# Channel mixing's moving operands placed at multiples of 64 bytes, weights left 32 bytes off, and GpSimd's first loads one head pair later

## The chip, the cores and the metric

The kernel runs on one core of a Trainium2 chip. The metric is the device time of one execution in microseconds (us). TensorE (PE in the profile) multiplies: a weight load (LDWEIGHTS, PEld in the profile) brings the stationary operand into the array, and a matmul streams the moving operand past it, one column after the other. VectorE (DVE), ScalarE (ACT) and GpSimd (POOL) do elementwise work; SyncE (SP) issues DMA transfers, and so do GpSimd and ScalarE. Tiles lie in SBUF, where each of the 128 partitions has its own bytes; an address here means the byte offset within a partition. Matmul results go to PSUM.

## The reference

All inputs and the output are float64 or float32 arrays that the kernel reads as 32-bit words; shapes are batch 4, 12 heads of 64, sequence 448, width 768.

```python
scores = q @ k^T / 8 - log(448)                  # sigmoid attention, per head
x  = sigmoid(scores) @ v                         # heads side by side: 4 x 448 x 768
u  = x + (x^T @ U @ V)^T                         # token mixing of rank 32
u  = u + relu(u @ w_ch1) @ w_ch2                 # channel mixing, 768 -> 3072 -> 768
th = u @ w_theta
u2 = u + w_tok_r @ (u * cos(th)) + w_tok_i @ (u * sin(th))
out = u2 + relu(u2 @ w_ch)
```

## The kernel before, in words

**Arithmetic.** Most products use float32r operands split into a high and a low part, and each product is three matmuls: high by high, high by low, low by high.

**Attention (lines 592 to 647).** The loop over `p` handles 24 pairs of heads. `load_qk(p)` fetches a pair's q and k in four quarters each, `TK(p)` and `TQ(p)` transpose them on DVE into `kT_t[p]` and `qT_t[p]`, `K_hi`, `K_lo` and the function that `TQ` returns split them. `QK(p, c)` makes three chunks of scores (9 matmuls for each of two heads, side by side in the array), ACT takes the sigmoid, `AV` multiplies by v (in plain float32), `QK_rest` and `AV_rest` do the 64 keys left over, once per two pairs. `load_qk(p + 4)` at the end of a turn keeps q and k four pairs ahead. All these q and k transfers but the first pair's are issued by SP.

**Early conversion.** Meanwhile ten float64 matrices of the later stages are loaded on GpSimd's queue and converted to float32 in small steps: `esteps` lists all steps of all jobs in order, 48 in all, and `early_step()` does the next one. The order of the jobs is that of the `queue(...)` calls (lines 495 to 504): U0, V0, one block of w_ch1, U1, V1, one of w_ch2, and four more weight blocks. Before a job's first step (`size`, line 139) the load of the job two places further on is issued. The first two loads are issued in the loop at `p == 0`, behind a small copy on GpSimd that reads `kT_t[1]` and so holds GpSimd until that transpose is done (line 606). Calls of `early_step` begin at `p == 1`: two in each turn, and one more in turns 4 and 6.

**Channel mixing (from line 652).** It goes over 12 blocks `i` of the hidden width and 4 batches `b`. `ch1(i, b)` (lines 664 to 666) has the weights `w1` stationary and `uh`, `ul` (the split u) moving, 448 columns; `ch2(i, b)` (lines 686 to 688) has `w2` stationary and `gh`, `gl` (the split hidden layer) moving, 448 columns. Each has 36 matmuls, and each matmul has a weight load of its own. The matmuls of one `ch2` run behind the `ch1` of the next batch, so that ACT and DVE have time to make `gh` and `gl`.

**Where the tiles lie.** Pools are stacks: left pools grow upward from low addresses, right ones downward from the top. The allocator gives each tile a multiple of 32 bytes. Every large tile here has a size that is a multiple of 256 bytes, so a pool's start fixes the place of all its tiles relative to lines of 64 bytes. `X` begins at 17088, a multiple of 64. The small tile `warm` behind it takes 32 bytes, so that the weight rings of `wpool` begin at 60128, which is 32 past a multiple of 64, and so does every tile of the left pools above it: `cv` (conversion), `gpool` (`gh`, `gl` from 121568), the attention pools `ap`, `ap1`, `ap2`, then `u23` (`uh`, `ul` of batches 2 and 3 from 135904) and `sp`. The right stack ends at 229344, also 32 past a multiple, and `u01` (`uh`, `ul` of batches 0 and 1, from 186336) lies there. So in the kernel before each moving operand and each stationary one of attention, channel mixing and the stages behind it starts 32 bytes past a multiple of 64; matmul operands at multiples of 64 are those of the transposes alone (`X`, `ident`).

Of the kernel before, what the change touches and what calls it, by code (L numbers as in the profile page):

```python
# [11 lines left out]
F32 = mybir.dt.float32  # L12
# [12 lines left out]
def tile_kernel(  # L25
# [15 lines left out]
    nc = tc.nc  # L41
# [4 lines left out]
    P = 128  # L46
# [23 lines left out]
    def runs(b, n0, n1):  # L70

        if b % 2 == 0:
            return [(n0, n0, n1 - n0)]
        got = []
        if n0 < REM:
            e = min(n1, REM)
            got.append((n0, n0 + S - REM, e - n0))
            n0 = e
        if n0 < n1:
            got.append((n0, n0 - REM, n1 - n0))  # L80
        return got
# [19 lines left out]
    def pool(name, side="left", space=None):  # L101
        st = ExitStack()
        kw = dict(name=name, bufs=1, side=side, reuse_waits="tile")
        if space is not None:
            kw["space"] = space
        return st.enter_context(tc.tile_pool(**kw)), st


    def hi_act(o, i):
        nc.scalar.activation(o, i, AF.Copy)  # L110
# [7 lines left out]
    def lo_dve(o, i, h):  # L118
        nc.vector.tensor_sub(o, i, f(h))
# [63 lines left out]
    def fin_split(dest, key, name, tag):  # L183
        def fin(a, t):
            dest[key] = ring(tag, name)
            split(dest[key], a, lo_pool if "sp" in late else lo_dve)
        return fin

    def loader():
        return nc.sync if "sp" in late else nc.gpsimd  # L190

    def load_row(src, r0):
        def dma(s):
            loader().dma_start(out=s.rearrange("p n t -> p (n t)"), in_=src[r0:r0 + P, :])
        return dma

    def conv_w1(i, j):
        c0 = (i * FB + j) * P

        def dma(s):  # L200
            loader().dma_start(
                out=s.rearrange("p (k f) t -> p k (f t)", k=NK),
                in_=w1_w[:, 2 * c0:2 * (c0 + P)].rearrange("(k p) f -> p k f", p=P),
            )
        return Conv(f"w1_{i}_{j}", P, DM, dma, fin_split(w1_t, (i, j), f"w1_{i}_{j}", "w1"))

    def conv_w2(i, j):
        name = f"w2_{i}_{j}"
        return Conv(name, P, DM, load_row(w2_w, (i * FB + j) * P), fin_split(w2_t, (i, j), name, "w2"))
# [56 lines left out]
    def conv_U(par):  # L266
        def dma(s):
            sv = s.rearrange("p (k r) t -> p k (r t)", k=NS)
            for g in range(P // R):
                for n, t, m in runs(par, 0, S):  # L270
                    nc.gpsimd.dma_start(
                        out=sv[g * R:(g + 1) * R, n // R:(n + m) // R],
                        in_=U_w[t:t + m, :].rearrange("(k j) w -> j k w", j=R),
                    )

        def dest():
            return u_in[:, par].rearrange("p k r -> p (k r)").bitcast(U32)
        return Conv(f"U{par}", P, NS * R, dma, None, dest=dest)

    def conv_V(par):  # L280
        def dma(s):
            sv = s.rearrange("p n t -> p (n t)")
            for g in range(P // R):
                for n, t, m in runs(par, 0, S):
                    nc.gpsimd.dma_start(
                        out=sv[g * R:(g + 1) * R, 2 * n:2 * (n + m)], in_=V_w[:, 2 * t:2 * (t + m)]
                    )

        def fin(a, t):
            hi_act(vh[:, par], a)  # L290
            lo_dve(vl[:, par], a[:2 * R], vh[:2 * R, par])
        return Conv(f"V{par}", P, S, dma, fin)

    cv, cv_st = pool("cv")
    gpool, gpool_st = pool("gpool")
    late = {}

# [64 lines left out]
    kT_t, qT_t = {}, {}  # L362

    def TK(p):
        x = ap2.tile([P, S], F32, tag="kT", name=f"kT_{p}", bufs=2)
        nc.vector.transpose(out=x, in_=k_t.pop(p).rearrange("p k j -> p (k j)"))
        kT_t[p] = x
# [4 lines left out]
    def K_hi(p):  # L372
        h_ = ap2.tile([P, NFULL, P], F32R, tag="kh", name=f"kh_{p}", bufs=2)
        l_ = ap2.tile([P, NFULL, P], F32R, tag="kl", name=f"kl_{p}", bufs=2)
        kk_t[p] = (h_, l_)
        hi_act(h_, by_chunks(p))
# [10 lines left out]
    def QK(p, c):  # L387
        ps = ps_b.tile([P, 2, 512], F32, tag="sc", name=f"sc_{p}_{c}", bufs=2)[:, :, :S]
        (kh, kl), (qh, ql) = kk_t[p], qq_t[p]
        for n, (a, b) in enumerate(((kh, qh), (kh, ql), (kl, qh))):  # L390
            for h in range(2):
                sl = slice(h * D, (h + 1) * D)
                nc.tensor.matmul(ps[:, h], a[sl, c], b[sl], start=n == 0, stop=n == 2)  # L393
        A_t[p, c] = weigh(ps, "A", f"A_{p}_{c}", 4)
# [94 lines left out]
    def queue(name, job):  # L489
        if seq:  # L490
            seq[-1].next = job
        seq.append(job)
        plan[name] = job

    queue("U0", conv_U(0))
    queue("V0", conv_V(0))
    queue(("w1", 0, 0), conv_w1(0, 0))
    queue("U1", conv_U(1))
    queue("V1", conv_V(1))
    queue(("w2", 0, 0), conv_w2(0, 0))  # L500
    queue(("w1", 0, 1), conv_w1(0, 1))
    queue(("w2", 0, 1), conv_w2(0, 1))
# [56 lines left out]
    warm = cpool.tile([P, 1], F32, name="warm")  # L559
# [22 lines left out]
    def split_u(b, p, d0, d1, *los):  # L582
        if d0 == 0:
            uh_t[b] = p.tile([P, NK, S], F32R, name=f"uh{b}")
            ul_t[b] = p.tile([P, NK, S], F32R, name=f"ul{b}")
        for d in range(d0, d1):
            x = X[:, d, b * S:(b + 1) * S]
            hi_act(uh_t[b][:, d], x)
            los[d % len(los)](ul_t[b][:, d], x, uh_t[b][:, d])
# [8 lines left out]
    for p in range(NP):  # L598
        nx = p + 1 < NP
        QK(p, 0)  # L600
        QK(p, 1)
        if nx:
            TK(p + 1)
            TQ(p + 1)()
        if p == 0:
            nc.gpsimd.tensor_copy(warm, kT_t[1][:, :1])
            seq[0].load()
            seq[1].load()
        if p:
            AV(p - 1, 0)  # L610
            AV(p - 1, 1)
        if nx:
            K_hi(p + 1)
        if p:
            early_step()
        if nx:
            K_lo(p + 1)
        b, r = divmod(p - 2 - NH, NH)
        if b >= 0 and r == 0:
            U1(b, ap)  # L620
            u1_lo()
        b, r = divmod(p - 3 - NH, NH)
        if b >= 0 and r < NK // 2:
            ps = ps_a.tile([P, 2, 512], F32, tag="ux", name=f"h_{b}_{r}")
            U2(b, 2 * r, ps, (vh[:, b % 2], vl[:, b % 2]))
        QK(p, 2)
        if not nx:
            ap2_st.close()
            u01, u01_st = pool("u01", "right")
            split_u(0, u01, 0, 3, lo_dve)  # L630
        if p % 2 == 0:
            QK_rest(p // 2)
        if p:
            AV(p - 1, 2)
        if p % 2:
            AV_rest(p // 2)
        if p > 1:
            XT(p - 2)
        if p in (4, 6):
            early_step()  # L640
        if p % 2 == 0 and p + 2 < NP:
            load_v(p // 2 + 1)
        if p + 4 < NP:
            load_qk(p + 4)
        if p:
            early_step()
    split_u(0, u01, 3, NK, lo_dve)
    while esteps:
# [6 lines left out]
    def ch1(i, b, js=range(FB)):  # L655
        if js[0] == 0:
            g_t[i, b] = ps_g.tile([P, FB, 512], F32, tag="g", name=f"g_{i}_{b}", bufs=2)
        ps = g_t[i, b]
        for j in js:
            wh, wl = w1_t[i, j][:, 0], w1_t[i, j][:, 1]  # L660
            for kk in range(NK):
                o = ps[:, j, :S]
                sl = slice(kk * P, (kk + 1) * P)
                nc.tensor.matmul(o, wh[:, sl], uh_t[b][:, kk, :], start=kk == 0, stop=False)  # L664
                nc.tensor.matmul(o, wh[:, sl], ul_t[b][:, kk, :], start=False, stop=False)  # L665
                nc.tensor.matmul(o, wl[:, sl], uh_t[b][:, kk, :], start=False, stop=kk == NK - 1)  # L666
        if js[-1] != FB - 1:
            return
        h = gpool.tile([P, FB, S], F32R, tag="gh", name=f"gh_{i}_{b}", bufs=2)
        l = gpool.tile([P, FB, S], F32R, tag="gl", name=f"gl_{i}_{b}", bufs=2)  # L670
        nc.scalar.activation(h, ps[:, :, :S], AF.Relu)  # L671
        nc.vector.scalar_tensor_tensor(  # L672
            out=l, in0=ps[:, :, :S], scalar=0.0, in1=f(h), op0=ALU.max, op1=ALU.subtract
        )
        g_t[i, b] = (h, l)
# [24 lines left out]
    XT(NP - 2)  # L700
    XT(NP - 1)
    split_u(1, u01, 0, NK, lo_pool, lo_dve)
    ch1(0, 0)
    ch1(0, 1, (0,))
    U1(B - 1, uv)
# [67 lines left out]
    sp_st.close()  # L773
    u23_st.close()
    gpool_st.close()
    cv_st.close()
    ps_g_st.close()
    ps_y_st.close()
# [216 lines left out]
```

## Time and profile before

| | |
|---|---|
| median of three runs | 1170.56 us (1170.17 to 1170.56) |
| the profiled execution | 1170.08 us |
| its span, first to last instruction | 1168.3 us |
| PE busy | 1155.3 us (99%) |
| DVE, ACT, POOL busy | 647.9, 360.9, 189.5 us |
| mean DMA rate over the span | 85 GB/s |

PE's busy time holds the modelled pipeline of a matmul (a matmul of 448 columns is shown with some 365 ns, and they overlap), so it doesn't say how fast PE goes. What says it is the distance from one matmul's start to the next one's, or the number of matmuls in a stretch. The profiled execution lies 1.8 us above its span, and the median 0.5 us above the profiled execution.

### The profile page before, as it was taken

Reading aid. Unit: us, or ns where it says so; the run is one execution under the profiler, and the core shown is the slowest. Engines: PE = TensorE matmul, PEld = TensorE weight load, DVE = VectorE, ACT = ScalarE, POOL = GpSimd, SP = SyncE. Lnnn points to the kernel's source line nnn. Section 1 sums busy time; section 2 is a strip of 40 time slices with the busy share of each in tenths; the row PEclk is TensorE's granted clock in tenths of the full one; section 3 lists DMA queues with packets and bytes.
Section 4 is the critical chain, followed back from the end, with each engine's and each line's share of the span. In section 5 each row is a group of like instructions: output and inputs, shape, how many; then the busy total and the mean of one; then the engine's idle time right before and its main releaser. Section 6 shows DMA issues by size and latency. Waiting matters only on the chain.

```text
span 1168.3 us, 15638 instructions
## 1 busy us (share of the span) xinstructions
PE 1155.3 (99%) x6414; PEld 1000.5 (86%) x6414; DVE 647.9 (55%) x805; ACT 360.9 (31%) x465; POOL 189.5 (16%) x136
## 2 busy tenths in 40 slices
PE   7999999999999999999999999999999999999998
PEld 3444458999999999999999999999999999999997
DVE  4777873445554555455545556565375542732443
ACT  5878872212221222122212222222125341630110
POOL 2300012211111111111111122222002321410000
PEclk9999999999999999999999999999999999999999
DMA  9887830113231323132313242424431000120444
GB/s 168 165 162 141 161 83 1 55 54 97 51 133 54 97 52 131 54 97 53 130 54 98 66 140 61 155 61 156 164 138 52 1 1 1 45 119 1 61 64 66
DMA packets 183719, 100.57 MB, mean 86 GB/s; under 512 B 151232, under 2 KB 174656, under 8 KB 183520
## 3 DMA queue, kind: packets, MB, share of 16 engines
q1 hardware_dynamic: 156800, 87.95, 28.3%
q0 software_dynamic: 2368, 8.24, 2.5%
q10 hardware_dynamic: 24480, 3.39, 2.0%
q8 instruction: 50, 0.82, 0.3%
q14 instruction: 21, 0.17, 0.0%
HBM read 81.40 MB, written 18.15 MB: 85 GB/s over the span
## 4 chain that ended last, share of the span: by engine, by line
PE 97%; DMA 1%; SPq 1%; DVE 1%; ACT 0%; issue 0%; ACTq 0%
PE g L664 10%; PE g L666 10%; PE g L665 10%; PE y L686 10%; PE y L688 10%; PE y L687 10%; PE av L419 5%; PE sc L393 4%; PE y L877 3%; PE y L876 3%; PE y L878 3%; PE th L799 3%; PE th L803 3%; PE th L800 2%; PE wc L958 2%; PE wc L959 2%
## 5 line engine op out<-in xcount | busy, mean ns | idle before, releaser
L690 DVE TENSOR_TENSOR X<-y,X 128x896 f32<-128x896 f32 x144 | 157.1, 1091 | 114.9 <-PE y L688 113.5
L686 PE MATMUL y<-gh,w 128*128 128x448 f32 x576 | 210.7, 366 | 0.2 <-DVE X L690 0.2
L664 PE MATMUL g<-uh,w 128*128 128x448 f32 x576 | 210.7, 366 | 0.0
L687 PE MATMUL y<-gl,w 128*128 128x448 f32 x576 | 210.4, 365 | 0.0
L688 PE MATMUL y<-gh,w 128*128 128x448 f32 x576 | 210.4, 365 | 0.0
L666 PE MATMUL g<-uh,w 128*128 128x448 f32 x576 | 210.4, 365 | 0.0
L665 PE MATMUL g<-ul,w 128*128 128x448 f32 x576 | 210.4, 365 | 0.0
L671 ACT ACTIVATE gh<-g 128x896 fp32r<-128x896 f32 x48 | 44.1, 919 | 390.8 <-PE g L666 390.8
L672 DVE SCALAR_TENSOR_TENSOR gl<-g,gh 128x896 fp32r<-128x896 f32 x48 | 52.4, 1092 | 183.8 <-ACT gh L671 183.8
L113 POOL TENSOR_TENSOR w<-ca_w,w 128x768 fp32r<-128x768 f32 x42 | 77.8, 1853 | 432.0 <-ACT w L110 432.0
L664 PEld LDWEIGHTS g<-uh,w 128*128 128x128 f32 x576 | 108.2, 188 | 9.8 <-ACT uh L110 0.7
L686 PEld LDWEIGHTS y<-gh,w 128*128 128x128 f32 x576 | 108.2, 188 | 9.7 <-issue 1.1
L688 PEld LDWEIGHTS y<-gh,w 128*128 128x128 f32 x576 | 108.2, 188 | 8.6
L666 PEld LDWEIGHTS g<-uh,w 128*128 128x128 f32 x576 | 108.2, 188 | 8.6
L687 PEld LDWEIGHTS y<-gl,w 128*128 128x128 f32 x576 | 108.2, 188 | 8.6
L665 PEld LDWEIGHTS g<-ul,w 128*128 128x128 f32 x576 | 108.2, 188 | 8.5
L384 ACT ACTIVATE A<-sc,bias_s 128x896 f32<-128x896 f32 x72 | 72.2, 1006 | 23.4 <-PE sc L393 12.8
L419 PE MATMUL av<-A,v 128*64 128x448 f32 x288 | 65.2, 561 | 0.0
L876 PE MATMUL y<-tok,zh 128*128 128x448 f32 x168 | 61.7, 367 | 0.0
L877 PE MATMUL y<-tok,zh 128*128 128x448 f32 x168 | 61.5, 366 | 0.0
L113 POOL TENSOR_TENSOR zl<-t,zh 128x768 fp32r<-128x768 f32 x23 | 42.7, 1880 | 115.4 <-ACT zh L110 115.4
L878 PE MATMUL y<-tok,zl 128*128 128x448 f32 x168 | 61.4, 366 | 0.0
(139 smaller groups left out, 1634.6 us busy)
## 6 DMA issues: line engine op xcount, KB each, us to landing
ws_w<-in_moe_w_ch_dram SPq DMA_DIRECT2D x40, 768.0 KB, 4.4
ws_w<-in_moe_w_ch_dram POOLq DMA_DIRECT2D x8, 768.0 KB, 5.9
k<-in_k_dram SPq DMA_DIRECT2D x94, 56.0 KB, 2.7
q<-in_q_dram SPq DMA_DIRECT2D x93, 56.0 KB, 3.1
ws_th<-in_moe_w_theta_dram SPq DMA_DIRECT2D x6, 768.0 KB, 4.3
th_d<-sp_th SPq DMA_DIRECT2D x6, 768.0 KB, 4.1
ws_wc<-in_moe_w_ch_dram SPq DMA_DIRECT2D x6, 768.0 KB, 4.7
wc_d<-sp_wc SPq DMA_DIRECT2D x6, 768.0 KB, 4.5
```

What stands on the lines that cost most here:

```text
L113: nc.gpsimd.tensor_sub(o, a, b)
L419: nc.tensor.matmul(ps[h * D:(h + 1) * D, :S], v_t[p // 2][:, 2 * (p % 2) + h, c, :], A_t[p, c][:, h, :], start=c == 0 and p % 2 == 0, stop ...
L664: nc.tensor.matmul(o, wh[:, sl], uh_t[b][:, kk, :], start=kk == 0, stop=False)
L665: nc.tensor.matmul(o, wh[:, sl], ul_t[b][:, kk, :], start=False, stop=False)
L666: nc.tensor.matmul(o, wl[:, sl], uh_t[b][:, kk, :], start=False, stop=kk == NK - 1)
L686: nc.tensor.matmul(o, wh[:, sl], gh[:, j, :], start=j == 0, stop=False)
L687: nc.tensor.matmul(o, wh[:, sl], gl[:, j, :], start=False, stop=False)
L688: nc.tensor.matmul(o, wl[:, sl], gh[:, j, :], start=False, stop=j == FB - 1)
L690: nc.vector.tensor_add(x, ps[:, :, :S], x)
L876: nc.tensor.matmul(o, zh[:, sl], tok_h[:, i, :], start=n == 0, stop=False)
L877: nc.tensor.matmul(o, zh[:, sl], tok_l[:, i, :], start=False, stop=False)
L878: nc.tensor.matmul(o, zl[:, sl], tok_h[:, i, :], start=False, stop=n == NZ - 1)
```

## The change

Two tiles of 32 bytes that nothing reads or writes are added. The first, in a new left pool `pad` above `cv`, moves all later left pools up by 32 bytes until it is closed with `cv` ahead of the last stages: `gpool`, `ap`, `ap1`, `ap2`, `u23` and `sp` now begin at multiples of 64 (`gh` at 121600, `uh` of batch 2 at 135936). The second, in `u01`, moves that pool down by 32 bytes, to 186304, a multiple of 64, and the small `uv` below it. `cpool`, `wpool` and `cv` stay, and so do the pools of the stages behind channel mixing (`tokhl`, `xr`, `zp`).

The order of the early jobs becomes U0, V0, U1, V1, and then the weight blocks. GpSimd's first loads wait for `kT_t[2]` in turn 1 in place of `kT_t[1]` in turn 0, the first `early_step` comes in turn 2, and the two steps lost there are made up in turns 8 and 10.

```diff
     cv, cv_st = pool("cv")
+    pad, pad_st = pool("pad")
+    pad.tile([P, 1], F32, name="pad_l")
     gpool, gpool_st = pool("gpool")
...
     queue("U0", conv_U(0))
     queue("V0", conv_V(0))
-    queue(("w1", 0, 0), conv_w1(0, 0))
     queue("U1", conv_U(1))
     queue("V1", conv_V(1))
+    queue(("w1", 0, 0), conv_w1(0, 0))
...
-        if p == 0:
-            nc.gpsimd.tensor_copy(warm, kT_t[1][:, :1])
+        if p == 1:
+            nc.gpsimd.tensor_copy(warm, kT_t[2][:, :1])
             seq[0].load()
             seq[1].load()
...
-        if p:
+        if p > 1:
             early_step()
...
-        if p in (4, 6):
+        if p in (4, 6, 8, 10):
             early_step()
...
-        if p:
+        if p > 1:
             early_step()
...
     split_u(1, u01, 0, NK, lo_pool, lo_dve)
+    u01.tile([P, 1], F32, name="pad_r")
...
     gpool_st.close()
+    pad_st.close()
     cv_st.close()
```

## Rows read from the trace of the kernel before

**Rows 1.** The page: span, and each engine's busy time, share and instructions.
```profile
span 1168.3 us, 15638 instructions
PE 1155.3 (99%) x6414; PEld 1000.5 (86%) x6414; DVE 647.9 (55%) x805; ACT 360.9 (31%) x465; POOL 189.5 (16%) x136
```

**Rows 2.** The page: the chain that ended last, by engine and by line.
```profile
PE 97%; DMA 1%; SPq 1%; DVE 1%; ACT 0%; issue 0%; ACTq 0%
PE g L664 10%; PE g L666 10%; PE g L665 10%; PE y L686 10%; PE y L688 10%; PE y L687 10%; PE av L419 5%; PE sc L393 4%; PE y L877 3%; PE y L876 3%; PE y L878 3%; PE th L799 3%; PE th L803 3%; PE th L800 2%; PE wc L958 2%; PE wc L959 2%
```

**Rows 3.** Stretch of channel mixing: busy time and instructions by engine, PE clock, DMA.
```profile
225.25:867.70 642.45, 642.25 (x3170) 594.99 (x3169) 363.93 (x376) 133.10 (x164) 100.15 (x53) 1.00 0.30 95
```

**Rows 4.** Timeline of PE in channel mixing: start, duration, instruction; eleven matmuls, first and last.
```profile
299.66 0.36 PE L665 MATMUL g<-ul,w 128*128 128x448 f32 x1
...
301.69 0.36 PE L666 MATMUL g<-uh,w 128*128 128x448 f32 x1
```

**Rows 5.** The same at channel mixing's end: seven matmuls, first and last.
```profile
870.65 0.37 PE L688 MATMUL y<-gh,w 128*128 128x448 f32 x1
...
871.89 0.37 PE L688 MATMUL y<-gh,w 128*128 128x448 f32 x1
```

**Rows 6.** The same for the projection, 384 columns: seven matmuls, first and last.
```profile
899.99 0.33 PE L800 MATMUL th<-th_r,xh 128*128 128x384 f32 x1
...
901.03 0.33 PE L800 MATMUL th<-th_r,xh 128*128 128x384 f32 x1
```

**Rows 7.** The chain in order of time, end of attention: start, length, what.
```profile
160.14 1.65 PE av L419 x8
...
165.42 2.41 PE av L419 x12
```

**Rows 8.** Groups by line: count, busy us and mean ns of one, idle before them.
```profile
L664 PE MATMUL g<-uh,w 128*128 128x448 f32 x576 | 210.7, 366 | 0.0
...
L690 DVE TENSOR_TENSOR X<-y,X 128x896 f32<-128x896 f32 x144 | 157.1, 1091 | 114.9 <-PE y L688 113.5 <-POOL ul L113 1.3
...
L688 PEld LDWEIGHTS y<-gh,w 128*128 128x128 f32 x576 | 108.2, 188 | 8.6
...
L672 DVE SCALAR_TENSOR_TENSOR gl<-g,gh 128x896 fp32r<-128x896 f32 x48 | 52.4, 1092 | 183.8 <-ACT gh L671 183.8
...
L419 PEld LDWEIGHTS av<-A,v 128*64 128x64 f32 x288 | 16.5, 135 | 30.8 <-issue 29.7 <-DMA q<-in_q_dram 0.9 <-ACT uh L110 0.2
```

**Rows 9.** Timeline of PE in the first pairs; idle time before in brackets.
```profile
19.54 0.47 PE L393 MATMUL sc<-qh,kh 64*128 64x448 f32 x2
...
26.16 0.97 PE L402 MATMUL sl<-qT,kT 64*64 64x448 f32 x4 [1.77 <-DVE qT L354]
...
28.66 0.74 PE L393 MATMUL sc<-qh,kh 64*128 64x448 f32 x2
...
35.23 0.47 PE L393 MATMUL sc<-qh,kh 64*128 64x448 f32 x2
...
40.92 0.47 PE L393 MATMUL sc<-qh,kh 64*128 64x448 f32 x2
```

**Rows 10.** Timeline of DVE: the transposes of the third k and the fourth q.
```profile
13.31 0.64 DVE L366 STREAM_TRANSPOSE kT<-k 128x448 f32<-128x448 f32 x1
...
25.46 0.65 DVE L354 STREAM_TRANSPOSE qT<-q 128x448 f32<-128x448 f32 x1 [4.86 <-DMA q<-in_q_dram]
```

**Rows 11.** Timeline of POOL: the copy that holds it, and its first loads.
```profile
10.50 0.18 POOL L606 COPY warm<-kT 128x1 f32<-128x1 f32 x1 [7.16 <-DVE kT L366]
10.98 2.66 POOL L271 DMA_DIRECT2D ws_U<-in_moe_U_dram  x4 [0.30 <-issue]
13.63 2.00 POOL L285 DMA_DIRECT2D ws_V<-in_moe_V_dram  x4
15.62 0.88 POOL L201 DMA_DIRECT2D ws_w<-in_moe_w_ch_dram  x1
```

**Rows 12.** Stretches, columns as in rows 3: PE's clock after the stall, and the DMA's.
```profile
26.20:30.70 4.50, 4.50 (x20) 2.19 (x20) 4.13 (x8) 2.00 (x3) 0.65 (x2) 0.62 0.68 110
...
20.00:25.00 5.00, 4.39 (x30) 1.76 (x26) 0.60 (x1) 3.77 (x5) 0.00 (x0) 1.00 1.10 256
```

## The prediction

> **What bounds the kernel.** I read the page's busy times first: PE 99% busy, the next engine 55% [rows 1]. Then the chain that ended last: 97% of it is PE, and six lines of channel mixing are 10% each [rows 2]. So only two things can move the time: how fast PE takes its matmuls, and the few gaps in which it has none. For the speed I counted matmuls in a stretch, since their shown durations overlap: 642.45 us hold 3170 of them, 202.7 ns each, at granted clock 1.00, the 2.4 GHz level [rows 3]. Ten steps in the timeline say the same (301.69 − 299.66 = 2.03 us) [rows 4]. But 448 columns at 2.4 GHz take 448 / 2.4 = 186.7 ns. Each matmul therefore loses 16.0 ns to something that isn't the clock or a wait.
>
> Three more places show what that depends on. At the end of channel mixing the step is (871.89 − 870.65) / 6 = 206.7 ns, by the same lines with operands at the same places in a line [rows 5]. In the projection with 384 columns it is (901.03 − 899.99) / 6 = 173.3 ns, 13.3 over the 160.0 of its columns [rows 6]. And attention's float32 product hardly loses anything: twelve of its records take 2.41 us and eight 1.65, so the four between them, two steps of two side by side, take 0.76 us, 0.38 a step or 190 ns for each of the two passes of 448 columns that such a step's length stands for [rows 7]. Its weight loads are also the shorter ones, 135 ns against 188, and there is one for two passes [rows 8]. So the loss goes with full-rate streams beside full weight loads, which fits two reads of SBUF getting into each other's way; and 206.7 and 173.3 ns are 31 and 26 times 6.67 ns, the time of 16 columns, or 64 bytes. This rhythm is why I take a place within 64 bytes to matter at all.
>
> **The change, part by part.**
>
> *Moving operands to multiples of 64.* All six lines with 576 matmuls each [rows 8] get an aligned moving operand, 3456 matmuls; the weights stay 32 off. No row of before has a full-rate matmul of these shapes whose moving operand is aligned: all are 32 off. So the price of one is bounded from its neighbours. Below: attention's 190 ns [rows 7], 12.7 less (the rounding of its rows leaves 2.5 ns either way). Above: the other rhythm, 206.7, 4.0 more [rows 5]. Between them I take one step of 6.67 ns less: 448 columns are 1792 bytes, 28 lines of 64 when aligned and 29 when they start 32 off, and a line is the unit in which rows 5 and 6 come. 3456 × 6.67 = 23.0 us, all of it on PE's chain. The ends are −43.9 and +13.8 us.
>
> The Trainium skill (TensorE: Matmul & The Clock Gate, Back-to-back issue gap) gives N / 2.4 + 2.5 ns for an isolated warm matmul, 189.2 for 448 columns; attention's steps agree with it, channel mixing's 202.7 don't. By that figure 13.5 ns of each matmul could be won, 46.7 us in all. The same page (Step-by-step: what each phase is for) says that the moving operand and the weights come through two independent read ports, so where they lie relative to each other should not matter; that speaks against any gain, and it is the first rival below. The 16.0 ns that come and go with the weight loads speak against the page, though no row here shows a different placing.
>
> *Attention moves too*, moving and stationary operands both to multiples of 64. Its score matmuls are at full rate: 24 pairs × 9 steps = 216 steps × 6.67 = 1.4 us; ends −2.7 and +0.9 by the bounds above. The float32 product has nothing left to win.
>
> *The other engines read and write at the new places.* DVE takes 1091 ns for 896 columns of `X`, which lies at a multiple of 64, and 1092 for as many of `gl` and `gh`, which lie 32 off [rows 8]. I cost this at nothing.
>
> *GpSimd's first loads.* Here the trace has a stall. DVE waits 4.86 us for the fourth pair's q and can transpose it only at 25.46 [rows 10]; PE idles 1.77 us for that, and then finds its clock down: from 26.20 to 30.70 the mean granted clock is 0.62, between the 1.2 GHz and the 2.4 GHz level [rows 9, 12]. From QK start to QK start the third pair takes 28.66 − 19.54 = 9.12 us, the fourth 35.23 − 28.66 = 6.57, and the fifth 40.92 − 35.23 = 5.69 [rows 9]. The stall costs 3.43 + 0.88 = 4.3 us. In that time GpSimd has U0, V0 and a block of w_ch1 in flight, issued from 10.98 to 16.5 [rows 11], beside q and k. After the change the copy waits for the third k's transpose at 13.31, done 13.95 [rows 10], 3.6 us later than the copy's release before, and the third load is U1, in place of 768 KB of weights (U1 has 448 KB). At the 256 GB/s of 20 to 25 us [rows 12] the 328 KB less are 1.3 us; the later start takes more away. I expect the q some 2 us earlier, about the length of PE's gap, and take 3.0 of the 4.3 us, because the rest hangs on whether the clock still falls. Ends: 4.3 won, or 0, when U1's eight transfers hold up the next pair's q instead.
>
> What is queued behind: GpSimd has nothing else to do there; the later steps of U and V land on ACT and DVE one turn later, and nothing needs U0 before turn 8. SP's q and k queue isn't moved past anything. The two steps put into turns 8 and 10 hold 0.4 to 1.2 us of ACT or DVE work beside a PE that is the bound. These I cost at nothing; the cover is the four pairs of lookahead.
>
> **The sum.** 23.0 + 1.4 + 3.0 = 27.4 us from the profiled 1170.1, which is 1142.7; the median lies 0.5 higher, so 1143.
>
> **The rivals.**
>
> *Placing does nothing* (chance 0.27). If weights and columns meet at any offset, since one runs through its lines faster than the other, moving the start by 32 only moves where they meet. For it: 202.7 and 206.7 come with the same placing [rows 4, 5], so it is time that decides which. Against it: nothing in these rows. Then the first loads alone count: 1170.1 − 3.0 + 0.5 = about 1167.5, and 1170 if that stall stays; 0.15 of the chance lies below 1168.2 and 0.12 within 0.2%.
>
> *The whole excess goes* (0.19). With moving and weights in opposite halves of 64 bytes they may never meet. Each step falls to attention's 190: 43.9 + 3.0 us, and 1170.1 − 46.9 + 0.5 = 1124. For it: attention's 190 [rows 7]. Against it: the projection loses 13.3 ns with the same weight load and fewer columns [rows 6], so the loss isn't a fixed number of meetings per load.
>
> *Slower by the other rhythm* (0.20). The new offset may settle PE in the 206.7 ns step that it already shows [rows 5], with every weight load in the way of one more line. 3456 × 4.0 = 13.8 us more, less 3.0 from the first loads: 1181. It decides from 0.9 ns per matmul on, where the 3.0 us are used up. Against it: that rhythm lasts for short stretches only, and then gives way.
>
> **The numbers.** My forecast, one line per matmul, has 0.34. Below it lies 0.19, and above it 0.27 and 0.20. About 0.2%, 2.3 us, is what a measurement of this kernel can tell from no change. Faster: 0.34 + 0.19 + 0.15 = 0.68; same 0.12; slower 0.20. The range leaves out the slower rival and takes the others in: from 1119, which is the whole excess with the full 4.3 us (1122) and a nanosecond a matmul of the rounding of rows 7, to 1171, a first-loads stall that stays.
>
> **What would show it.** Matmuls in a stretch of channel mixing, as in rows 3: near 196 ns each for my forecast, 202.7 if placing does nothing, 190 or 206.7 for the others. The projection, whose placing isn't touched, must keep its 173.3. The step from the third pair's QK to the fourth's should fall from 9.1 towards 5.7 us, with no dip of the clock. I am wrong if the step stays at 202.7, or if it changes by anything that isn't about one 64-byte unit; and in the first loads, if the fourth q lands no earlier.

## The result, and the profile after

The change made the kernel slower: median 1177.34 us (six executions, 1176.99 to 1181.16) against 1170.37 for the kernel before on the same chips, a ratio of 1.0067 [1.0057, 1.0078]. The forecast was 1143, the range 1119 to 1171. Of the rivals the nearest is the third, "slower by the other rhythm", at 1181. One execution of *sched_only* below (1265 us, mean granted clock 0.85) and one of *start_only* (4029 us) are left out of their ratios.

The profiled execution took 1181.16 us, 1.8 above its span. The page's first rows look like [rows 1] but for PE:

```profile
span 1179.4 us, 15636 instructions
PE 1166.9 (99%) x6414; PEld 1001.3 (85%) x6414; DVE 647.5 (55%) x805; ACT 361.2 (31%) x465; POOL 189.2 (16%) x136
```

The stretch of channel mixing that answers to [rows 3] (stretch, its length, then busy us and instructions of PE, PEld, DVE, ACT, POOL, PE's clock, DMA share, GB/s):

```profile
225.90:877.00 651.10, 651.10 (x3162) 594.81 (x3161) 361.76 (x373) 133.69 (x164) 100.11 (x53) 1.00 0.29 93
```

651.10 / 3162 is 205.9 ns a matmul, where [rows 3] gave 202.7, again at clock 1.00 and without idle time. All of channel mixing, from its first matmul to the projection's first, takes 167.8 to 875.2 us before and 168.1 to 886.3 after: 707.4 and 718.2, 10.8 us more. Every later stage takes what it took before, to 0.1 us. So of the 11.1 us between the two profiled executions 10.8 are in channel mixing.

There are two new steps in it. PE's timeline in a `ch1` of batch 3 and in one of batch 0, the first and last of 36 matmuls each (start, duration, instruction):

```profile
270.34 0.37 PE L666 MATMUL g<-uh,w 128*128 128x448 f32 x1
...
277.57 0.37 PE L668 MATMUL g<-uh,w 128*128 128x448 f32 x1
...
285.22 0.37 PE L666 MATMUL g<-uh,w 128*128 128x448 f32 x1
...
292.38 0.36 PE L668 MATMUL g<-uh,w 128*128 128x448 f32 x1
```

35 steps take 7.23 us in the one, 206.6 ns each, and 7.16 in the other, 204.6. By exact starts it is 206.7 in `ch1` of batches 2 and 3 and in `ch2` (206.3 behind a block of the other kind, and 204.4 in its first two blocks), and 204.5 in `ch1` of batches 0 and 1. The border between the two is that of the pools: the first read what the left pad moved up by 32 bytes, the second what the right pad moved down by 32.

The stall of the first pairs [rows 9] is gone from its place. Pairs are counted from 0 from here on, so the prediction's third pair is pair 2. The QK starts of pairs 2, 3 and 4, and the clock from pair 3 to pair 4:

```profile
18.32 0.47 PE L395 MATMUL sc<-qh,kh 64*128 64x448 f32 x2
...
24.64 0.47 PE L395 MATMUL sc<-qh,kh 64*128 64x448 f32 x2
...
30.40 0.47 PE L395 MATMUL sc<-qh,kh 64*128 64x448 f32 x2
...
24.64:30.40 5.76, 5.76 (x41) 2.47 (x39) 2.52 (x6) 4.23 (x6) 1.45 (x3) 1.00 0.76 135
```

The step from pair 3 to pair 4 is 5.76 us, where it was 6.57, and from pair 2 to pair 3 it is 6.32 where it was 9.12. At pair 4 the kernel is 4.8 us ahead. 1.2 us of that are there at pair 2 already (18.32 against 19.54), ahead of the stall: the first k is transposed 1.2 us earlier, before any of the loads that the change puts off. DVE before and after:

```profile
6.61 0.65 DVE L366 STREAM_TRANSPOSE kT<-k 128x448 f32<-128x448 f32 x1 [5.71 <-DMA k<-in_k_dram]
...
5.38 0.65 DVE L368 STREAM_TRANSPOSE kT<-k 128x448 f32<-128x448 f32 x1 [4.47 <-DMA k<-in_k_dram]
```

But pair 4 to 5 then takes 6.97 (5.69 before), 7 to 8 6.61 (5.69) and 8 to 9 10.98 (8.13), and by pair 9 it is 0.3 us behind. Pair 8 has the old stall over again, first on DVE, then on PE, then in the clock:

```profile
52.37 0.65 DVE L368 STREAM_TRANSPOSE kT<-k 128x448 f32<-128x448 f32 x1 [2.75 <-DMA k<-in_k_dram]
...
55.50 0.47 PE L395 MATMUL sc<-qh,kh 64*128 64x448 f32 x2 [0.67 <-ACT X L110]
...
57.18 0.59 PE L395 MATMUL sc<-qh,kl 64*128 64x448 f32 x2 [0.64 <-DVE kl L119]
...
57.00:60.00 3.00, 2.82 (x12) 1.54 (x14) 2.56 (x7) 1.01 (x1) 0.55 (x1) 0.56 0.84 225
```

A late k, two gaps of 0.67 and 0.64 us, and a mean granted clock of 0.56 between 57 and 60 us, between the 1.2 and the 2.4 GHz level.

### The profile page after: what moved, and what is told of

It reads as the page before. It is cut to its first block, busy times and chain, and to the rows that moved or that the text cites. A ratio compares the mean times of both kernels' runs of the same rounds, so it can differ in the third digit from the quotient of the medians.

```text
span 1179.4 us, 15636 instructions
## 1 busy us (share of the span) xinstructions
PE 1166.9 (99%) x6414; PEld 1001.3 (85%) x6414; DVE 647.5 (55%) x805; ACT 361.2 (31%) x465; POOL 189.2 (16%) x136
## 3 DMA queue, kind: packets, MB, share of 16 engines
q1 hardware_dynamic: 156800, 87.95, 27.1%
## 4 chain that ended last, share of the span: by engine, by line
PE 96%; DMA 1%; DVE 1%; ACT 1%; POOL 0%; issue 0%; SPq 0%; DVEq 0%; ACTq 0%; POOLq 0%
PE y L688 10%; PE g L666 10%; PE y L689 10%; PE y L690 10%; PE g L667 10%; PE g L668 10%; PE av L421 4%; PE sc L395 3%; PE y L881 3%; PE y L882 3%; PE y L880 3%; PE th L803 3%; PE th L807 2%; PE th L804 2%; PE wc L962 2%; PE wc L963 2%
## 5 line engine op out<-in xcount | busy, mean ns | idle before, releaser
L692 DVE TENSOR_TENSOR X<-y,X 128x896 f32<-128x896 f32 x144 | 157.1, 1091 | 121.0 <-PE y L690 121.0
L674 DVE SCALAR_TENSOR_TENSOR gl<-g,gh 128x896 fp32r<-128x896 f32 x48 | 52.4, 1092 | 188.1 <-ACT gh L673 188.1
```

The source lines that it names most:

```text
L692: nc.vector.tensor_add(x, ps[:, :, :S], x)
```

## The experiments

**Theories.** A: the price of a matmul comes from where the moving operand lies relative to its weights, and opposite halves of 64 bytes are a bad place; then the pads alone make the kernel slower. B: the place does nothing, PE just falls into one rhythm or the other, and it is the start that decides. C: the new order of the first loads is what costs.

### Each part alone

Three kernels on one chip, where before takes 1169.90.

*pads_only* is the kernel after without its changes of order:

```diff
+    pad, pad_st = pool("pad")
+    pad.tile([P, 1], F32, name="pad_l")
...
+    u01.tile([P, 1], F32, name="pad_r")
...
+    pad_st.close()
```

> The kernel before with the two pads alone. The theory that the pads cost all: channel mixing at 206 to 207 ns a matmul, 3456 x 3.1 to 4 ns, 11 to 14 us slower than before (1181 to 1184). The rival that the order of the early jobs brings PE into the slower rhythm: as before, 1170, with 202.7 ns.

Measured: 1178.08 (1177.73 to 1178.42), ratio 1.0072 [1.0055, 1.0089]. The same stretch:

```profile
225.90:877.00 651.10, 651.05 (x3161) 593.50 (x3160) 362.07 (x375) 133.60 (x164) 100.15 (x53) 1.00 0.29 94
```

206.0 ns a matmul, 718.0 us of channel mixing. The pads alone carry the whole loss.

*sched_only* is the kernel after without its pads: order of the jobs, GpSimd's start, the moved steps.

```diff
-    queue(("w1", 0, 0), conv_w1(0, 0))
     queue("U1", conv_U(1))
     queue("V1", conv_V(1))
+    queue(("w1", 0, 0), conv_w1(0, 0))
...
-        if p == 0:
-            nc.gpsimd.tensor_copy(warm, kT_t[1][:, :1])
+        if p == 1:
+            nc.gpsimd.tensor_copy(warm, kT_t[2][:, :1])
...
-        if p:
+        if p > 1:
             early_step()
...
```

> The changed kernel without the two pads: the early jobs' order and their start one pair later alone. The theory that the pads cost all of the loss: channel mixing steps of 202.7 ns as before, the stall before the fourth pair gone, 3 to 4 us faster than before (about 1166.5). The rival that the first loads lose what they gain (in the profiled run of the changed kernel pair 8 to 9 took 10.98 us in place of 8.13): within 1 us of before, 1170.

Measured: 1172.03, ratio 1.0018 [1.0008, 1.0028]. So the new order alone isn't worth 3.0 us; it costs some 2 (0.9 to 3.3 by the interval).

*all_aligned* moves the weights to multiples of 64 as well: one small tile behind `warm` lifts all left pools by 32, and a pad in `u01` as in the change.

```diff
     warm = cpool.tile([P, 1], F32, name="warm")
+    cpool.tile([P, 1], F32, name="pad_c")
...
+    u01.tile([P, 1], F32, name="pad_r")
```

> The kernel before with one pad of 32 bytes behind the small tile warm and one in u01: weights and moving operands of attention and channel mixing all at multiples of 64, so they keep their place relative to each other; in the projection the moving weights are at a multiple of 64 and the stationary operand stays 32 off, in the second token mixing the other way round; the last channel product has both at multiples of 64. If the relative place counts: channel mixing and the last product 202.7 ns as before, the projection 177 or so in place of 173.3 and token mixing near 206.5; in all about 1173. If the moving operand's own place counts: channel mixing and the last product near 206.5, the projection slower, token mixing 202.7; about 1183. If a straddled 64-byte line costs by itself: channel mixing faster than 202.7.

Measured: 1178.60, ratio 1.0076 [1.0061, 1.0091], as slow as the change. `ch1` of batches 0 and 1 stands at 202.1 ns. `ch2`, and `ch1` of batches 2 and 3, stand at 206.7, though moving operand and weights lie at equal places, as in the kernel before, where that gave 202.7. So does the last product (first and last of 41 matmuls, 8.27 / 40 = 206.8 ns):

```profile
1099.64 0.37 PE L959 MATMUL wc<-uh,wc_r 128*128 128x448 f32 x1
...
1107.91 0.37 PE L960 MATMUL wc<-ul,wc_r 128*128 128x448 f32 x1
```

The stages between have the moving operand 32 bytes off the stationary one, and react: token mixing, 32 below, goes from 203.4 to 204.4 ns, and the projection, 32 above, from 173.3 to 176.7. (Modulo 256 `ch1` of batches 0 and 1 doesn't keep its place either: `u01` went down to 186304, the weights up to 60160, which puts the moving operand 192 past its weights. The table of *micro_starts* below has 202.2 there.) So a place within 64 bytes isn't the whole of it, and the same relative place can have two rhythms; why this kernel has the slower one in all those blocks isn't shown. "Align everything" is no cure.

One thing is faster in the kernels that put the attention tiles at multiples of 64, whatever PE does: the transfers of q and k into them. The queue that carries nearly all of them, before and after (packets, MB, share of 16 DMA engines over the span):

```profile
q1 hardware_dynamic: 156800, 87.95, 28.3%
...
q1 hardware_dynamic: 156800, 87.95, 27.1%
```

The share is 26.6 to 27.1% in *pads_only*, *all_aligned* and the two profiles of the kernel after, and 28.1 to 28.3% in seven profiles of kernels whose attention tiles lie 32 off; the first k is transposed at 5.38 to 5.79 us in the four and at 6.54 to 6.70 in the seven. *place64* and *place64_all* below, which move the same tiles by 64 bytes, are among the seven.

### Matmuls alone

*micro_places* is 45 runs of 36 such matmuls, each with its weight load, on one large tile, one run behind the other; weights and moving operand start so many bytes past a multiple of 256, and a short matmul ahead of each run varies its start.

```python
def segment(wo, mo, n=448, cols=128, count=36):
    w0, m0, m1 = W + wo // 4, M + mo // 4, M2 + mo // 4
    for t in range(count):
        kk, j = divmod(t % 18, 3)
        mm(w0 + kk * 128 + (768 if j == 2 else 0), (m1 if j == 1 else m0) + kk * n, n, cols)
```

> A kernel of matmuls alone (it computes nothing of the reference): 128 rows, 128 weight columns, 448 moving columns, in runs of 36 with the pattern of channel mixing (high, low, high), each matmul with its own weight load; the runs differ in where weights and moving operands start. Corners, weights/moving in bytes past a multiple of 64, three starts each. If the place of one relative to the other counts: 32/32 and 0/0 near 202.7 ns a matmul, 32/0 and 0/32 near 206.5. If it is the moving operand's own place: 32/32 and 0/32 near 202.7, 32/0 and 0/0 near 206.5. If place does nothing and the start sets the rhythm: 202.7 and 206.7 turn up in all four. Further runs move the moving operand in 16, 48, 64, 96 to 224 bytes (a period of 64 in the first two theories), take 512, 384, 320 and 256 columns, and take 64 weight columns, where by both the loss should shrink to a few ns over 186.7.

Measured, as the mean step over the last 24 of each run's 36, in ns (all at clock 1.00):

| weights / moving, bytes past 256 | 448 columns |
|---|---|
| 32/32, 0/0 (three starts each) | 202.7 in all six |
| 32/0 (three starts) | 204.4, 204.5, 203.3 |
| 0/32 (three starts) | 200.0, 200.0, 204.5 |
| 32/64 | 206.7 |
| 32/96, 0/64 | 200.0, 200.0 |
| 32/128, 0/96 | 205.3, 205.4 |
| 0/4, 0/8 | 208.3, 205.7 |

Runs with the same distance, moving less weights, mostly agree wherever both lie: 32/96 and 0/64 are both 64 apart, 32/128 and 0/96 both 96. The exceptions are 32 apart, with 200.0, 204.5 and 206.7 by the start, and 16 apart (200.0 at 32/48, 202.2 at 0/16); the next kernel was made for them. With 32/32 and other lengths the step is 226.7 ns for 512 columns, 173.3 for 384, 146.7 for 320 and 120.0 for 256: columns / 2.4 GHz plus 13.3 each time, and only 448 has 16.0. And with 64 weight columns in place of 128 it is 202.2 in all three places tried (32/32, 32/0, 0/0). So at equal places most of the excess is 13.3 ns that shrink neither with the columns nor with the weights, and the few ns around them hang on the place.

*micro_starts* asks how much is the place and how much the start: one distance after the other, with many lengths of the short matmul ahead.

```python
for d in (0, 32, -32):
    for n in range(64, 184, 6):
        shift(n)
        segment(0, d, count=24)
for d in (16, 64, 96, 128, 160, 192):
    for n in (64, 78, 92, 108, 122, 136, 152, 166):
        shift(n)
        segment(0, d, count=24)
```

> Matmuls alone again (nothing of the reference is computed), weights at a multiple of 64 bytes, runs of 24 matmuls of 448 columns, each run behind one matmul of 64 to 178 columns that shifts its start. Moving operand at 0, +32 and -32 bytes from the weights' place, 20 starts each; then at +16, +64, +96, +128, +160 and +192, 8 starts each. The theory that the place alone sets the step: each place has one step (0: 202.7; the first places measured gave 200.0 or 206.7 at +32 and 203.3 to 204.5 at -32). The theory that PE falls into one of several steady rhythms, and that the place only sets which ones there are: the same place shows several steps, 200.0, 202.7 and 206.7 among them, and the start decides.

Measured, mean step over the last 15 of each run's 24:

| distance, modulo 256 bytes | runs | step, ns |
|---|---|---|
| 0 (kernel before) | 20 | 202.7 in 19, 206.7 in 1 |
| +32 (`ch2`, and `ch1` of batches 2, 3 after) | 20 | 206.7 in 18, 204.4 in 1, 200.0 in 1 |
| -32 (`ch1` of batches 0, 1 after) | 20 | 204.5 in 15, 203.3 in 5 |
| +16 | 8 | 200.0 in 6, 202.2 in 2 |
| +64, +160 | 8 each | 200.0 in all |
| +96 / +128 / +192 | 8 each | 205.3 / 204.0 / 202.2 in all |

The same eight starts at 64, 96, 128 and 160 bytes, as stretches that hold their 200 matmuls (the counts of PE take in a neighbour at the ends; stretch, length, busy us and instructions of PE, PEld, ACT, POOL, clock, DMA):

```profile
373.66:413.01 39.35, 39.35 (x201) 36.89 (x200) 0.00 (x0) 0.00 (x0) 1.00 0.00 0
413.01:453.31 40.30, 40.30 (x201) 36.93 (x200) 0.00 (x0) 0.00 (x0) 1.00 0.00 1
453.31:493.34 40.03, 40.03 (x202) 36.96 (x200) 0.00 (x0) 0.00 (x0) 1.00 0.00 0
493.34:532.70 39.36, 39.36 (x201) 36.93 (x200) 0.00 (x0) 0.00 (x0) 1.00 0.00 1
```

The distance says which rhythms there are, and the start picks one where there are several. A is right in its first half (the price goes with the relative place), but not with 64 bytes as the measure; of B it holds that the start decides where a distance has several steps. A distance of 0 has a second rhythm, 206.7, which is what [rows 5] and *all_aligned* show. By this table the change's blocks should stand at 204.5 (a quarter of the matmuls) and 206.7 (three quarters), as they nearly all do.

*nudged* asks whether a start can be changed in the kernel itself: 22 short matmuls in `ch1`, whose sum the next matmul overwrites.

```diff
+                if i and b % 2 == 0 and j == 0 and kk == 0:
+                    n = 64 + 6 * (2 * (i - 1) + b // 2)
+                    nc.tensor.matmul(o[:, :n], wh[:, sl], uh_t[b][:, 0, :n], start=True, stop=True)
```

> The kernel before, no operand moved; in channel mixing from block 1 on, one short matmul of 64 to 190 columns is added ahead of every second batch's first product (22 in all, about 0.1 us each; its result is overwritten). The theory of places: 202.7 ns a matmul throughout, 2 to 3 us slower in all. The theory of rhythms: after some of the nudges PE goes over to 206.7 ns and stays there until the next, so that some stretches have 202.7 and others 206.7; 5 to 10 us slower in all.

Measured: 1173.57 (one execution; before 1170.66 beside it), 2.9 us slower, as the theory of places had it. 21 of the 22 stretches between two nudges stay at 202.7. One falls into 206.7 and stays there until the next nudge:

```profile
284.52 0.20 PE L666 MATMUL g<-uh,w 128*128 128x76 f32 x1
...
290.62 0.37 PE L669 MATMUL g<-uh,w 128*128 128x448 f32 x1
...
291.86 0.37 PE L669 MATMUL g<-uh,w 128*128 128x448 f32 x1
```

(291.86 − 290.62) / 6 = 206.7. A nudge is a dear way to a rhythm, and at distance 0 no start here gave less than 202.7.

### The theory's own place

*place64* uses the table: both pads are larger, so that every moving operand of channel mixing lies 64 bytes past its weights, modulo 256 (left pools up by 64, `u01` down by 192). The order of the first loads is that of the kernel before.

```diff
+    pad.tile([P, 16], F32, name="pad_l")
...
+    u01.tile([P, 48], F32, name="pad_r")
```

> The kernel before with larger pads: 64 bytes above cv and 192 in u01, so that in channel mixing each moving operand starts 64 bytes past its weights' place, counted modulo 256. The theory that the distance between the two sets PE's rhythm: 200.0 ns a matmul as in all 8 starts of the kernel of matmuls alone, 2.67 ns x 3456 = 9.2 us less, about 1161. If what was measured with PE alone doesn't hold beside the other engines and semaphores: 202.7 or 206.7 ns, 1170 to 1184.

Measured: 1161.43 (1160.34 to 1164.73), ratio 0.9932 [0.9916, 0.9947]. The stretch holds 634.10 / 3170 = 200.0 ns a matmul, and 39 steps of the timeline give 7.80 / 39 = 200.0:

```profile
225.90:860.00 634.10, 633.82 (x3170) 593.77 (x3169) 365.22 (x377) 133.25 (x164) 100.40 (x53) 1.00 0.30 96
```

*place64_all* does the same for token mixing and the last product (`tok`, `xr` and `zp`).

```diff
+                tokhl.tile([P, 32], F32, name="pad_t")
+                xpad.tile([P, 32], F32, name="pad_x")
...
+    zpad.tile([P, 16], F32, name="pad_z")
```

> As place64, and the second token mixing and the last channel product with their moving operands 64 bytes past the stationary ones too (pads of 64 bytes below zp, 128 beside tok, 128 above xr; the projection keeps its places). The theory of the distance: 200.0 ns there as well, (504 + 396) x 2.7 = 2.4 us more won, about 1158.7, and 173.3 ns in the projection as before.

Measured: 1158.56 (1157.91 to 1159.44), ratio 0.9903 [0.9888, 0.9918]. Token mixing goes from 203.4 to 200.1 ns, the last product from 202.7 to 200.0 (41 steps, 8.20 us):

```profile
1099.65 0.36 PE L970 MATMUL wc<-uh,wc_r 128*128 128x448 f32 x1
...
1107.85 0.36 PE L969 MATMUL wc<-ul,wc_r 128*128 128x448 f32 x1
```

This is the fastest of all kernels here. Both times were worked out ahead from steps in the table, and both came out within half a microsecond.

### The first loads

*sched_again* is *sched_only* once more, for a profile, and *after_again* the kernel after once more.

> The changed kernel without the pads once more, for a trace at the full clock. Its time was 2 us above the kernel before. The theory that what the first loads gain is lost again in pairs 4 to 9, where the weight load now collides with q and k: channel mixing starts within 1 us of the kernel before's 167.8 us, its steps are 202.7 ns. The theory of rhythms: its steps are partly 206.7 ns.

> The changed kernel once more, since the execution that was profiled took 1181.2 us and four of the other five 1177.0 to 1177.4. If the 4 us are lost in attention: channel mixing starts near 164 us in an execution of 1177, in place of 168.1, and its steps are the same 206.4 ns. If the rhythm differs from one execution to the next: the start is the same and the steps are shorter.

Measured: 1171.37 and 1178.35 (before 1170.66). In *sched_again* the stall from pair 2 to pair 3 is gone, as foreseen, and two more stand behind it: pair 3 to 4 takes 8.25 us, 4 to 5 8.59, and channel mixing begins 1.3 us later than before (169.0). DVE, PE, GpSimd and the clock there:

```profile
28.74 0.65 DVE L366 STREAM_TRANSPOSE kT<-k 128x448 f32<-128x448 f32 x1 [3.58 <-DMA k<-in_k_dram]
32.20 0.65 DVE L354 STREAM_TRANSPOSE qT<-q 128x448 f32<-128x448 f32 x1 [2.82 <-DMA q<-in_q_dram]
...
33.42 0.47 PE L393 MATMUL sc<-qh,kh 64*128 64x448 f32 x2 [2.33 <-DVE qh L357]
35.10 0.47 PE L393 MATMUL sc<-qh,kl 64*128 64x448 f32 x2 [0.64 <-DVE kl L119]
...
19.21 1.17 POOL L271 DMA_DIRECT2D ws_U<-in_moe_U_dram  x2
...
25.09 2.32 POOL L271 DMA_DIRECT2D ws_U<-in_moe_U_dram  x4 [1.78 <-DMA ws_V<-in_moe_V_dram]
...
35.00:40.00 5.00, 4.90 (x22) 1.93 (x22) 3.31 (x8) 2.76 (x4) 3.33 (x7) 0.66 1.00 203
```

U1's eight transfers are issued from 19.21 to 27.4, beside the next pair's k and q; those are now the late ones, PE waits 2.33 and 0.64 us, and the clock is at 0.66 behind it. In *after_again* channel mixing begins at 165.5, 2.3 us earlier than before, with 718.0 us of channel mixing behind it. So the same kernel gains or loses some 2.6 us in its first nine pairs from one execution to the next.

*order_only* changes only the order of the `queue` lines and *start_only* only the waiting copy and the steps; each is one half of *sched_only*'s diff. Before takes 1170.25 beside them.

> The kernel before with the changed order of the early jobs alone (U1 and V1 ahead of the first weight block); the first loads start in turn 0 as before. If it was the weight block of 768 KB that held up the fourth pair's q: the stall of pair 3 shrinks and 1 to 3 us are won. If U1's eight transfers do the same harm to the next pair: within 1 us of before or up to 2 us slower.

> The kernel before with the later start of GpSimd's loads alone (third k's transpose, steps from turn 2); the order stays U0, V0, a weight block, U1, V1. If the stall only moves to the pair whose q and k the loads then meet: pair 3 takes 5.7 us, pair 4 or 5 the 8 to 9 us instead, and the time is within 1 us of before. If the later start is what wins: 2 to 4 us less.

Measured: 1171.13, ratio 1.0006 [0.9996, 1.0016], and 1173.94, ratio 1.0035 [1.0022, 1.0048]. In *order_only* pair 2 to 3 costs 7.89 us (9.12 before), but 4 to 5 6.46 and 6 to 7 7.58 (5.69 before): a smaller stall in three places. In *start_only* pair 2 to 3 is clean at 5.69, and then 3 to 4 takes 9.21 and 4 to 5 8.74, and channel mixing begins at 171.7. Its PE:

```profile
34.46 0.74 PE L393 MATMUL sc<-qh,kh 64*128 64x448 f32 x2 [3.27 <-DVE qh L357]
36.14 0.74 PE L393 MATMUL sc<-qh,kl 64*128 64x448 f32 x2 [0.37 <-DVE kl L119]
```

The later start moves the stall one pair on and makes it larger; the smaller load only spreads it.

## Why the prediction was wrong

*Reading the bound* was right: PE is busy all through, and the time moved with the step of its matmuls.

*"So the loss goes with full-rate streams beside full weight loads"* was the first wrong step. Halving the weight columns left 202.2 ns, and 13.3 of the 16.0 ns stay at every length from 256 to 512. Attention's 190 ns [rows 7], which served as the lower bound, belongs to another kind of product (plain float32), and no run shows that it is the step of a float32r stream without collisions. So the lower bound of −12.7 ns was no bound for these matmuls: the smallest step at any place tried is 200.0, 2.7 below 202.7. The rival "the whole excess goes" fell with it. What the 13.3 ns are wasn't found.

*The price of aligning* is the term that failed: −6.67 ns by 3456 was −23.0 us, and the runs gave +2.7 ns on 1728 matmuls of `ch1` and +3.5 on 1728 of `ch2`, 4.7 + 6.1 = +10.8 us, the 10.8 between the stages' starts. The error was to count the lines that a moving operand touches by itself. (206.7 and 173.3 are multiples of 6.67 ns; 202.7, which the step was taken off, isn't.) What counts is its distance from the weights, and the kernel before had 0 everywhere: its tiles at 60128, 121568, 135904 and 186336 are all 224 past a multiple of 256. The change made +32 and −32 of it. "Multiples of 64, weights 32 off" is a sentence on two places, and only their difference matters here.

*The upper bound*, +4.0 ns from [rows 5], held, and was nearly what three quarters of the matmuls got (206.3 to 206.7). That the same place shows two rhythms was in the rows; I put it into a rival at 0.20 and spoke against it with "lasts for short stretches only". At a distance of 0 it is the rare rhythm in *micro_starts* (1 of 20), at +32 it is the usual one (18 of 20), so how long it lasted before said nothing of how long it would last after. The rival was right that the new offset settles PE in that rhythm, for three quarters of the matmuls; that each weight load gets in the way of one more line isn't shown, and *all_aligned* has the same 206.7 at a distance of 0. Its 1181 is 3.7 us above the median; 3.0 of that are channel mixing, which lost 10.8 in place of 13.8 us. That its −3.0 for the first loads was near what the attention won (2.3 us in *after_again*) is luck: alone the new order costs time.

*"Placing does nothing"* is refuted by the four kernels that differ from the one before in places alone. The Trainium skill (TensorE: Matmul & The Clock Gate, Step-by-step: what each phase is for) gives the two operands independent read ports, which the prediction counted for that rival. The steps of 200.0 to 206.7 ns by distance disagree with the conclusion that I drew from it; whether it is the reads that meet, or something else that follows addresses, no run here shows. The estimate of 189.2 ns for an isolated matmul, from the same page of the Trainium skill (Back-to-back issue gap), wasn't reached at any place either: 200.0 is the least.

*Attention's −1.4 us* wasn't seen. Its moving and stationary operands moved together, so their distance stayed; pairs 10 to 23 take the same 6.69, 5.69 and 8.12 us to 0.02 in both traces.

*The other engines at nothing* was right for DVE: `X` takes 1091 ns and `gl` 1092, as before. But the sum left out the DMA engines, which write q and k at the new places too. With these at multiples of 64 the first k is transposed 0.8 to 1.3 us earlier, and channel mixing begins at 163.8 (*all_aligned*) and 165.5 (*pads_only*), where four kernels with the same order of loads and tiles 32 off begin it at 167.7 to 168.5.

*The first loads, −3.0 us*: right that the stall of the prediction's third pair would go (9.12 to 6.32, with the fourth q transposed at 22.14 in place of 25.46), wrong that the gain would stay. The end given for it, 0, "when U1's eight transfers hold up the next pair's q instead", fits what happened in *sched_again*, and it was an end too high: alone the new order costs 2.1 us (0.9 to 3.3). The wrong step was to price one stall and not ask how far ahead the next pairs' k and q are. They come a pair every 5.7 us, so a load moved by one pair meets the next one. With the pads beside it, the order's effect can't be told: 1.0067 with and 1.0072 without have overlapping intervals.

*Why the loss is smaller than channel mixing's*: the kernels with the pads lost 7.0 and 8.2 us by their medians where channel mixing lost 10.8 and 10.5. In *pads_only* an earlier start of channel mixing makes up the rest: it begins 2.2 us earlier, and 10.5 − 2.2 = 8.3 is the difference of the profiled spans (1176.6 and 1168.3). With the new order beside the pads it begins at 168.1 in one profile and 165.5 in the other, so what is won in the first pairs can be lost again by pair 9. That faster q and k transfers win it is read from these few profiles; no run was made for it.

*Open*: why the good distances are 64 and 160 and the steps repeat after 256 bytes (that they do rests on −32 and +224, with 203.3 in both, and on *place64*, whose −192 gives the 200.0 of +64); what the 13.3 ns are; and why a transfer is faster into a multiple of 64. A kernel with q and k at multiples of 64 and channel mixing at a distance of 64 wasn't run.

## What to carry to other kernels

Where PE is the bound and its step is over columns / 2.4 GHz, read the step at two or three lengths first: here 13.3 ns of it came at every length with the operands at equal places, no place took 448 columns below that, and only what lay above could be won by moving tiles. Look at the difference between the addresses of moving operand and weights, modulo 256 bytes, not at either's alignment, and measure it on bare matmuls with several starts: a single short run at +32 could have shown 200.0, as 0/32 did twice, where the usual step is 206.7. A load that is in the way of a steady stream of loads is not helped by a later start alone; ask which transfer it will meet next. And a pad moves every tile above it: ask of DMA's tiles, too, where they come to lie.

## What the runs showed of the hardware

- A float32r matmul of 128 by 128 weights takes columns / 2.4 GHz + 13.3 ns with its own weight load beside it and both operands at equal places modulo 256 (256, 320, 384 and 512 columns), and 448 columns take 13.3 to 20.0 more than 186.7 by the distance of its operands, 200.0 to 206.7; at 4 bytes it was 208.3, 21.6 more.
- At one distance there can be two steady rhythms (202.7 and 206.7 at 0), each held for hundreds of matmuls: the slower one holds through the 396 matmuls of *all_aligned*'s last product, the faster one through those of the same product before.
- With the moving operand 32 bytes below the weights, 384 and 320 columns kept their step (173.3 and 146.7 at 32/32, 32/0 and 0/0), while 512 lost 6.7 ns (233.3 at 32/0) and 256 won 1.7 (118.3). With it 32 above, 384 columns lost 3.3 (176.7, the projection of *all_aligned*).
- q and k land sooner in tiles at multiples of 64 bytes than in tiles 32 past one: for the same 156800 packets the queue's share of the DMA engines' time is 26.6 to 27.1% in four profiles and 28.1 to 28.3% in seven.
